# Top-32 attention and a gated feed-forward part on one core: weights used as they are split, half-batch groups, signs on ScalarE, sums divided out after the weighted values

## Chip, cores and metric

One core of a Trainium2 chip runs the whole kernel. The metric is device time in microseconds (us), lower is better, median of the runs. TensorE (PE in the profile) multiplies matrices, VectorE (DVE), ScalarE (ACT) and GpSimd (POOL) do the rest, and SyncE (SP) issues every DMA. PEld is TensorE's loading of weights, which overlaps its matmuls.

## What is computed

```python
scores = scale * np.matmul(q, k.transpose(0, 1, 3, 2))      # 8 batches, 8 heads, 576 x 576, depth 64
kth = np.partition(scores, -top_k, axis=-1)[..., -top_k:-top_k + 1]   # top_k = 32
scores = np.where(scores >= kth, scores, -1000000000.0)
attn = np.exp(scores - np.max(scores, axis=-1, keepdims=True))
attn = attn / (np.sum(attn, axis=-1, keepdims=True) + 1e-09)
x = (attn @ v) as 4608 rows x 512
gate = 1.0 / (1.0 + np.exp(-(x @ w_gate)))                  # w_gate, w_val 512 x 1536, in double precision
out = (gate * (x @ w_val) @ w_out).astype(np.float32)       # w_out 1536 x 512
```

## The kernel before, in words

The work is a list of 160 steps. A step is one tile of 128 query rows of a pair of heads (two head tiles, J = 2), or the last 64 rows of both heads in one tile (J = 1); there are 288 head tiles. Batches 0 and 1 go through in two halves (256 and 320 rows), batches 2 to 7 whole (576 rows): `groups`, line 55.

Per step, `scores` (L177) multiplies queries by keys, each as a leading part and a remainder, into PSUM, and ScalarE copies them out as `s` (L184). `select` finds each row's 32nd largest score on VectorE: the 8 largest of each of eight segments of 72 (L237), three rounds of 8 over those candidates (L241, L243), which give the 24th largest as a bound; a count of the scores that reach the bound (`over`, L248, which also writes 0 or 1 for each score); GpSimd takes `over` from `s` (L249), VectorE takes the 8 largest of what is left (L252) and picks the 32nd by the count (L253). ScalarE meanwhile takes the exponentials (L192). `normalise` masks and sums them on VectorE (L196), and ScalarE multiplies by one over the sum (L202). `turn` transposes the result on TensorE (L273, L278), ScalarE copies it to `et` (L274). For every two tiles `weigh` multiplies by the values: one 128-column matmul for the chunk that mixes both heads (L289), then pairs of 64-column matmuls, one for each head (L291, L292); ScalarE and GpSimd split the sum into two parts `xh`, `xl`.

The feed-forward part of a group (`ffn`) runs in units of at most 320 rows. A unit takes 432 matmuls: 12 times 24 with gate and value weights (`pz`, L331 to L333), each followed by tanh on ScalarE (L336), a multiply on VectorE (`gf`, L337) and a split into `gh`, `gl`; and 3 times 48 with the output weights (L351 to L353). Its weights come from DRAM through three buffers (L313), 18 loads of 1 MB for a group, shared by the two units of a 576-row group.

The weights arrive in double precision. `split_weights` (L98) turns all 18 tiles, as 36 halves, into two parts each and stores them to DRAM before any feed-forward work is written down; per half it takes three VectorE instructions (L126, L127, L130), ScalarE and GpSimd instructions, three matmuls (L134 to L136) and a store. Four halves can be in flight (`raws`, bufs=4), and the feed-forward pools take the memory of the split's pools afterwards.

What sets the order: the program writes the steps one after another, loads two to four steps ahead, and after each step as much of the feed-forward work as brings it to 640 rows behind the selection (`BEHIND`, `goal`). A scheduler then gives each engine a fixed sequence, in which feed-forward matmuls stand between those of the steps. Each engine runs its own sequence strictly in turn and waits on semaphores.

## Time and profile before

| what | value |
|---|---|
| median of 3 runs | 1690.8 us (1689.48 to 1691.35) |
| span of the profiled execution | 1685.6 us, 5.2 us under the median |
| PE busy, PEld busy | 1575.0 us (93%), 1398.7 us (83%) |
| DVE busy | 1521.8 us (90%) |
| ACT, POOL busy | 1166.2 us (69%), 1052.7 us (62%) |
| DMA | 297.37 MB, 176 GB/s over the span |

Only the profiled execution has rows, so terms are worked out against its 1685.6 us; the runs that were timed lie 5.2 us above it in the median. Busy time of PE is a model (matmuls overlap), so the distance from one matmul's start to the next says what a matmul costs, not its own duration.

### The profile page before, as it was taken

What the parts mean: (1) busy time and instruction counts of PE and PEld (TensorE: products, weight loads), DVE (VectorE), ACT (ScalarE), POOL (GpSimd) and SP (SyncE); (2) the same over time, 40 slices, a digit from 0 to 9 for tenths busy, and PEclk for the clock granted to TensorE, in tenths of its full rate; (3) what the DMA queues carried; (4) which work ended last, traced back from release to release, by engine and by line L of the source; (5) the groups of instructions that cost most, each with busy time, mean ns of one, the idle gap of its engine ahead of it and who ended that gap; (6) DMA issues with size and microseconds to landing.
All of it is one profiled execution on the core that took longest, in us unless ns stands there. A gap on an engine that the chain in (4) does not pass through costs nothing.

```text
span 1685.6 us, 36209 instructions
## 1 busy us (share of the span) xinstructions
PE 1575.0 (93%) x11506; PEld 1398.7 (83%) x11506; DVE 1521.8 (90%) x6802; ACT 1166.2 (69%) x2467; POOL 1052.7 (62%) x1187
## 2 busy tenths in 40 slices
PE   5665799999999989999999999999999999999998
PEld 2333598888989868998899999999999898999998
DVE  7999999999999999999999999999999999995000
ACT  7787777776777667776676767777776776765222
POOL 6766667767666766576764676576756675564233
PEclk8788899999999989999999999999999999999999
DMA  8777586756776543334433444434534353333543
GB/s 303 257 237 236 206 290 245 271 205 242 251 265 213 210 129 116 138 136 139 163 132 130 136 156 147 134 133 149 170 132 153 124 166 130 118 106 110 195 156 125
DMA packets 86026, 297.37 MB, mean 176 GB/s; under 512 B 9536, under 2 KB 38208, under 8 KB 62784
## 3 DMA queue, kind: packets, MB, share of 16 engines
q1 hardware_dynamic: 85824, 294.95, 51.1%
q8 instruction: 93, 1.52, 0.4%
q14 instruction: 109, 0.89, 0.2%
HBM read 266.60 MB, written 28.31 MB: 175 GB/s over the span
## 4 chain that ended last, share of the span: by engine, by line
PE 49%; DVE 35%; ACT 3%; issue 2%; POOL 1%; POOLq 0%; ACTq 0%; DVEq 0%
PE pz L332 8%; PE pz L331 8%; PE pz L333 8%; DVE e L196 7%; DVE cand L237 7%; DVE tops L252 5%; DVE over L248 5%; PE pss L177 5%; PE pt L273 4%; PE po L351 3%; PE po L353 3%; PE po L352 3%; DVE pick L253 3%; DVE tops L241 3%; PE po L292 3%; DVE cand L243 3%
## 5 line engine op out<-in xcount | busy, mean ns | idle before, releaser
L331 PE MATMUL pz<-xh,w 128*128 128x288 f32 (+2 forms) x1536 | 461.9, 301 | 3.1 <-DVE gf L337 1.5
L332 PE MATMUL pz<-xl,w 128*128 128x288 f32 (+2 forms) x1536 | 459.4, 299 | 0.1
L333 PE MATMUL pz<-xh,w 128*128 128x288 f32 (+2 forms) x1536 | 458.5, 299 | 0.0
L249 POOL TENSOR_TENSOR u<-s,over 128x1152 f32<-128x1152 f32 (+1 forms) x160 | 354.3, 2214 | 74.0 <-DVE over L248 70.2
L237 DVE MAX8 cand<-s 128x8 f32<-128x72 f32 x2304 | 355.3, 216 | 7.0 <-ACT s L184 6.7
L196 DVE SCALAR_TENSOR_TENSOR e<-s,st,e 128x576 f32<-128x576 f32 x288 | 300.8, 1065 | 0.1
L331 PEld LDWEIGHTS pz<-xh,w 128*128 128x128 f32 x1536 | 289.3, 188 | 9.0 <-issue 3.5
L332 PEld LDWEIGHTS pz<-xl,w 128*128 128x128 f32 x1536 | 289.2, 188 | 3.9 <-issue 3.5
L333 PEld LDWEIGHTS pz<-xh,w 128*128 128x128 f32 x1536 | 289.2, 188 | 2.7 <-issue 2.7
L202 ACT ACTIVATE e<-e,st 128x576 f32<-128x576 f32 x288 | 209.4, 771 | 83.1 <-DVE st L200 82.5
L339 POOL TENSOR_TENSOR gl<-gf,gh 128x288 fp32r<-128x288 f32 (+2 forms) x192 | 163.1, 850 | 153.7 <-ACT gh L338 145.8
L192 ACT ACTIVATE e<-s,st 128x576 f32<-128x576 f32 x288 | 210.2, 774 | 35.0 <-POOL st L190 34.1
L351 PE MATMUL po<-gh,w 128*128 128x288 f32 (+2 forms) x768 | 224.4, 302 | 6.3 <-DVE gf L337 3.9
L248 DVE TENSOR_SCALAR_CACHE_REDUCE over<-s,tops 128x576 bf16<-128x576 f32 x288 | 228.5, 798 | 1.1
L352 PE MATMUL po<-gl,w 128*128 128x288 f32 (+2 forms) x768 | 227.6, 299 | 0.6 <-POOL gl L339 0.5
L353 PE MATMUL po<-gh,w 128*128 128x288 f32 (+2 forms) x768 | 226.1, 297 | 0.0
L177 PE MATMUL pss<-k,qh 128*128 128x288 f32 (+2 forms) x672 | 199.7, 314 | 23.5 <-ACT s L184 16.4
L184 ACT ACTIVATE s<-pss 128x576 f32<-128x576 f32 x288 | 185.8, 645 | 47.2 <-PE pss L177 24.2
L252 DVE MAX8 tops<-u 128x8 f32<-128x576 f32 x288 | 204.3, 744 | 2.2 <-POOL u L249 1.4
L274 ACT ACTIVATE et<-pt 128x384 f32<-128x384 f32 x384 | 180.5, 491 | 35.5 <-PE pt L273 33.9
L273 PE MATMUL pt<-ident,e 128*128 128x128 f32 x1152 | 189.7, 281 | 7.7 <-ACT e L202 4.0
L177 PE MATMUL pss<-k,ql 128*128 128x288 f32 (+2 forms) x672 | 190.4, 302 | 0.4 <-POOL ql L159 0.4
(82 smaller groups left out, 3380.3 us busy)
## 6 DMA issues: line engine op xcount, KB each, us to landing
w<-ws SPq DMA_DIRECT2D x180, 1024.0 KB, 5.0
kraw<-in_k_dram SPq DMA_DIRECT2D x80, 288.0 KB, 3.2
qraw<-in_q_dram SPq DMA_DIRECT2D x160, 128.0 KB, 3.0
wraw<-in_w_dram SPq DMA_DIRECT2D x36, 512.0 KB, 5.0
ws<-wpair SPq DMA_DIRECT2D x36, 512.0 KB, 5.4
v<-in_v_dram SPq DMA_DIRECT2D x40, 352.0 KB, 3.8
out_dram<-acc SPq DMA_DIRECT2D x48, 144.0 KB, 2.3
out_dram<-acc SPq DMA_DIRECT2D x8, 160.0 KB, 4.1
```

The costliest lines, as they stand in the source:

```text
L177: nc.tensor.matmul(ps[:, half, o : o + n], x[:, h * P : (h + 1) * P], ks[h][:, k0 : k0 + n], start=t == 0, stop=t == len(todo) - 1,)
L196: nc.vector.scalar_tensor_tensor(e[:, j], s[:, j], kth[j], e[:, j], op0=ALU.is_ge, op1=ALU.mult, accum_out=st[:, 4 + j : 5 + j])
L237: nc.vector.max(cand[:, j, 8 * g : 8 * g + 8], s[:, j, g * SEG : (g + 1) * SEG])
L248: nc.vector.tensor_scalar(over[:, j], s[:, j], t, None, op0=ALU.is_ge, op1=ALU.add, accum_out=c)
L249: nc.gpsimd.tensor_tensor(u[:, :J], s[:, :J], over[:, :J], op=ALU.subtract)
L252: nc.vector.max(t, u[:, j])
L331: nc.tensor.matmul(ps, wt[:, u, 0, d], xh[:, cols], start=d == 0, stop=False)
L332: nc.tensor.matmul(ps, wt[:, u, 0, d], xl[:, cols], start=False, stop=False)
L333: nc.tensor.matmul(ps, wt[:, u, 1, d], xh[:, cols], start=False, stop=d == NP - 1)
L351: nc.tensor.matmul(ps, wt[:, e % 2, 0, f], gh, start=f == 0, stop=False)
L352: nc.tensor.matmul(ps, wt[:, e % 2, 0, f], gl, start=False, stop=False)
L353: nc.tensor.matmul(ps, wt[:, e % 2, 1, f], gh, start=False, stop=f == FG - 1)
```

## The change

- The two-part split is no longer a block of its own. `split_weight(idx, held)` splits one tile. Nine of the 18 are split during the eight steps of the first group: three of them straight into the feed-forward part's own weight buffers (`HELD`), six into DRAM (`LOADED`). The other nine are split when the first feed-forward unit asks for them, into its weight buffer, and also stored. Two halves can be in flight instead of four. The first scaling moves from ScalarE to VectorE, so VectorE has four instructions per half.
- All batches go in halves of 256 and 320 rows; a unit is a half, and each unit loads its own 18 weight tiles. Keys of a batch stay for its second half. `BEHIND` is 384 instead of 640, and the first unit may be written from 256 rows on.
- `over` on VectorE is replaced by a Sign on ScalarE that also sums the signs; the bound is read from a strip of saved bounds (`leads`) with its lower 16 bits left off. GpSimd multiplies instead of subtracting.
- ScalarE's multiply by one over the sum goes. GpSimd spreads that number over 128 columns (`inv`), TensorE transposes it (L329), ScalarE copies it out (`rs`), and VectorE multiplies it onto the weighted values (L335, L339).
- In `weigh` the pairs come first, from the last chunk down, and the mixed matmul last.

```diff
-    groups = [(b, *half) for b in range(2) for half in ((0, 2), (2, NT + 1))]
-    groups += [(b, 0, NT + 1) for b in range(2, B)]
+    groups = [(b, *half) for b in range(B) for half in ((0, 2), (2, NT + 1))]
-    BEHIND = 640
+    BEHIND = 384
+    HELD, LOADED = 3, 6
...
-    bk = ctx.enter_context(tc.tile_pool(name="bk", bufs=4))
+    bk = ctx.enter_context(tc.tile_pool(name="bk", bufs=2 * NP))
...
+    pre_pools = {n: pre.enter_context(tc.tile_pool(name=n, bufs=bufs)) for n, bufs in (("signs", 1), ("raw", 2), ("parts", 2))}
...
+    def split_weight(idx, held):
+        if held:
+            wt = pools["w"].tile([P, 2, 2, NP, P], F32R, tag="w", name=f"wsplit_{idx}")
+            ready[idx] = wt
...
-                    nc.scalar.activation(lead, top.bitcast(F32), AF.Copy, scale=2.0**-112)
+            nc.vector.tensor_scalar(lead, top.bitcast(F32), 2.0**-112, None, op0=ALU.mult)
...
-        for j in range(J):
-            nc.scalar.activation(e[:, j], e[:, j], AF.Copy, scale=st[:, 6 + j : 7 + j])
+        inv = bi.tile([P, P], F32, tag="inv", name=f"inv_{nm}")
+        nc.gpsimd.tensor_copy(
+            inv.rearrange("p (j d) -> p j d", j=J), st[:, 6 : 6 + J].unsqueeze(2).to_broadcast([P, J, P // J])
+        )
...
-            nc.vector.tensor_scalar(over[:, j], s[:, j], t, None, op0=ALU.is_ge, op1=ALU.add, accum_out=c)
-        nc.gpsimd.tensor_tensor(u[:, :J], s[:, :J], over[:, :J], op=ALU.subtract)
+            nc.scalar.activation(
+                under[:, j], s[:, j], AF.Sign, bias=bound, scale=-CUT, accum_out=sums[:, j : j + 1]
+            )
+        nc.gpsimd.tensor_tensor(u[:, :J], s[:, :J], under[:, :J], op=ALU.mult)
...
-            nc.tensor.matmul(po, mixed, et[:, 4, :n], start=True, stop=False)
-            for c in range(4):
-                nc.tensor.matmul(po[:D], vt[:, c], et[:, c, :n], start=False, stop=c == 3)
-                nc.tensor.matmul(po[D:], vt[:, 6 + c], et[:, 5 + c, :n], start=False, stop=c == 3)
+            for c in reversed(range(4)):
+                nc.tensor.matmul(po[D:], vt[:, 6 + c], et[:, 5 + c, :n], start=c == 3, stop=False)
+                nc.tensor.matmul(po[:D], vt[:, c], et[:, c, :n], start=c == 3, stop=False)
+            nc.tensor.matmul(po, mixed, et[:, 4, :n], start=False, stop=True)
...
+        for t, inv in enumerate(invs):
+            nc.tensor.transpose(rb[:, t * P : (t + 1) * P], inv, ident)
+        nc.scalar.activation(rs[:, :m], rb[:, :m], AF.Copy)
...
-        nc.scalar.activation(xf, po, AF.Copy)
+            nc.vector.tensor_tensor(xf, po, rs[:, :n], op=ALU.mult)
...
+            if not (general or idx in stored):
+                split_weight(idx, True)
...
+            goal = max(at - BEHIND, min(at - 2 * P, 2 * P))
```

TensorE's sequence before, in the middle of batch 3: a `weigh` (po) with its mixed matmul first.

```order
L289 MATMUL po_3_1_3_11270<-et_3_0_3_11104,v_5_3_10761 128x256
L291 MATMUL po_3_1_3_11270<-et_3_0_3_11104,v_5_3_10761 64x256
L292 MATMUL po_3_1_3_11270<-et_3_0_3_11104,v_5_3_10761 64x256
L291 MATMUL po_3_1_3_11270<-et_3_0_3_11104,v_5_3_10761 64x256
L332 MATMUL pz_4_2_3_0_0_11650<-xl_4_1_6591,w_4_11_11646 128x288
L177 MATMUL pss_4_0_0_1_11529<-k_6_0_1_11511,qh_4_0_0_11189 128x288
L177 MATMUL pss_4_0_0_1_11529<-k_6_0_1_11511,ql_4_0_0_11190 128x288
L177 MATMUL pss_4_0_0_1_11529<-k_6_0_1_11511,qh_4_0_0_11189 128x288
L177 MATMUL pss_4_0_0_1_11529<-k_6_0_1_11511,ql_4_0_0_11190 128x288
L333 MATMUL pz_4_2_3_0_0_11650<-xh_4_1_6590,w_4_11_11646 128x288
L292 MATMUL po_3_1_3_11270<-et_3_0_3_11104,v_5_3_10761 64x256
```

Other matmuls stand between the first and the second head's half of one chunk: the pair is broken. The end of a `weigh` at the same stage of the changed kernel (inv is the spread-out number, pt are the next transposes):

```order
L318 MATMUL po_3_3_2_11993<-et_3_2_2_11838,v_7_2_11458 64x256
L319 MATMUL po_3_3_2_11993<-et_3_2_2_11838,v_7_2_11458 64x256
L320 MATMUL po_3_3_2_11993<-et_3_2_2_11838,v_7_2_11458 128x256
L329 MATMUL po_3_3_2_11993<-ident_102,inv_3_2_2_11834 128x128
L329 MATMUL po_3_3_2_11993<-ident_102,inv_3_3_2_11976 128x128
L304 MATMUL pt_3_4_2_0_12146<-ident_102,e_3_4_2_12118 128x128 x3
L307 MATMUL pt_3_4_2_1_12152<-ident_102,e_3_4_2_12118 64x128
L377 MATMUL pz_6_1_1_0_0_12178<-xh_6_0_9627,w_6_5_12174 128x256
```

Four whole pairs, the mixed matmul and two transposes now stand together (in 62 of 64 `weigh`s; before, 59 of 64 had the pair broken).

TensorE's sequence before, where the first feed-forward unit (po2_0) ends and the second (pz_1) begins:

```order
L351 MATMUL po2_0_2_3_0_4346<-gh_0_2_3_0_4149,w_0_17_4327 128x256
L352 MATMUL po2_0_2_3_0_4346<-gl_0_2_3_0_4150,w_0_17_4327 128x256
L353 MATMUL po2_0_2_3_0_4346<-gh_0_2_3_0_4149,w_0_17_4327 128x256
L331 MATMUL pz_1_0_0_0_0_4441<-xh_1_0_1756,w_1_0_4437 128x320
L332 MATMUL pz_1_0_0_0_0_4441<-xl_1_0_1757,w_1_0_4437 128x320
```

The same place in the changed kernel:

```order
L396 MATMUL po2_0_2_3_0_3156<-gl_0_2_0_0_2525,wsplit_17_3104 128x256
L147 MATMUL wrest_17_1_3125<-wt_frac_17_1_3126,plus_159 128x512
L299 MATMUL pt_1_1_2_0_4140<-ident_102,e_1_1_2_4095 128x128 x3
L299 MATMUL pt_1_1_2_1_4145<-ident_102,e_1_1_2_4095 128x128 x3
L375 MATMUL pz_1_0_0_0_0_3682<-xh_1_0_1418,w_1_0_3678 128x320
L376 MATMUL pz_1_0_0_0_0_3682<-xl_1_0_1419,w_1_0_3678 128x320
```

The split of the last weight tile (wrest_17) now stands right ahead of the second unit; before, all 36 halves stood ahead of the first.

VectorE's sequence before, in the selection of batch 4 (`over` of one tile between rounds of others):

```order
L241 MAX tops_4_4_2_13958<-cand_4_4_2_13957 128x8
L248 TENSOR_SCALAR over_4_4_2_13963,counts_115<-s_4_4_2_13617,tops_4_4_2_13958 128x576
L237 MAX cand_4_0_3_14065<-s_4_0_3_13781 128x8 x2
L252 MAX tops_4_3_2_13795<-u_4_3_2_13799 128x8 x2
L237 MAX cand_4_0_3_14065<-s_4_0_3_13781 128x8 x6
```

And in the changed kernel, in batch 6:

```order
L266 MAX leads_119<-cand_6_0_2_19732 128x8
L279 MAX below_6_1_1_19549<-u_6_1_1_19554 128x8 x2
L219 RECIPROCAL st_6_0_1_19392<-st_6_0_1_19392 128x2
L381 SCALAR_TENSOR_TENSOR gf_11_0_0_0_19488<-gf_11_0_0_0_19488,pz_11_0_0_0_1_19475 128x320
L280 SCALAR_TENSOR_TENSOR pick_6_1_1_19552,kths_118<-wanted_107,sums_6_1_1_19551,below_6_1_1_19549 128x8
L335 TENSOR_TENSOR xf_6_1_0_19282<-po_6_1_0_19268,rs_6_1_0_19280 128x256
```

The pass over 576 scores is gone from VectorE, and the multiply onto the weighted values (xf) is there instead, once for two tiles.

## Rows read from the trace of the kernel before

**Rows 1.** The page's part 1: busy us (share of the span), instructions.

```profile
PE 1575.0 (93%) x11506; PEld 1398.7 (83%) x11506; DVE 1521.8 (90%) x6802; ACT 1166.2 (69%) x2467; POOL 1052.7 (62%) x1187
```

**Rows 2.** Windows of 50 us: length, each engine's busy us (instructions), PE clock, DMA share, GB/s.

```profile
150.00:200.00 50.00, 30.47 (x121) 18.63 (x121) 50.00 (x179) 37.62 (x71) 30.24 (x29) 0.86 0.59 202
...
550.00:600.00 50.00, 48.49 (x349) 44.30 (x349) 50.00 (x230) 34.82 (x73) 33.68 (x38) 1.00 0.60 212
600.00:650.00 50.00, 39.67 (x261) 30.72 (x260) 49.97 (x233) 33.31 (x70) 32.97 (x36) 0.86 0.36 113
650.00:700.00 50.00, 50.00 (x389) 46.28 (x388) 49.94 (x246) 40.03 (x86) 30.19 (x36) 1.00 0.41 138
...
1550.00:1600.00 50.00, 50.00 (x387) 47.80 (x386) 3.78 (x9) 13.79 (x35) 13.12 (x18) 1.00 0.49 172
```

**Rows 3.** TensorE in order of time: start us, duration us, instruction, count.

```profile
294.49 0.28 PE L353 MATMUL po<-gh,w 128*128 128x256 f32 x1
294.61 0.31 PE L331 MATMUL pz<-xh,w 128*128 128x320 f32 x1
...
295.35 0.31 PE L333 MATMUL pz<-xh,w 128*128 128x320 f32 x1
...
997.06 0.49 PE L273 MATMUL pt<-ident,e 128*128 128x128 f32 x3
997.38 0.60 PE L289 MATMUL po<-et,v 128*128 128x256 f32 x2
...
998.92 0.66 PE L278 MATMUL pt<-ident,e 128*128 128x128 f32 x4
...
1000.96 0.43 PE L292 MATMUL po<-et,v 128*64 128x256 f32 x1
...
1002.40 0.30 PE L281 MATMUL pt<-ident,e 128*64 128x128 f32 x1
...
1009.93 0.30 PE L351 MATMUL po<-gh,w 128*128 128x288 f32 x1
...
1010.72 0.29 PE L351 MATMUL po<-gh,w 128*128 128x288 f32 x1
...
1086.48 0.59 PE L289 MATMUL po<-et,v 128*128 128x256 f32 x2
...
1088.88 0.55 PE L278 MATMUL pt<-ident,e 128*128 128x128 f32 x3
```

**Rows 4.** VectorE in order of time: start us, duration us, instruction, count.

```profile
301.65 0.47 DVE L337 SCALAR_TENSOR_TENSOR gf<-gf,pz 128x320 f32<-128x320 f32 x1
...
1000.01 0.81 DVE L248 TENSOR_SCALAR_CACHE_REDUCE over<-s,tops 128x576 bf16<-128x576 f32 x1
...
1000.75 1.26 DVE L196 SCALAR_TENSOR_TENSOR e<-s,st,e 128x576 f32<-128x576 f32 x1
```

**Rows 5.** Groups by line: count | busy us, mean ns of one | idle before.

```profile
L248 DVE TENSOR_SCALAR_CACHE_REDUCE over<-s,tops 128x576 bf16<-128x576 f32 x288 | 228.5, 798 | 1.1
...
L337 DVE SCALAR_TENSOR_TENSOR gf<-gf,pz 128x288 f32<-128x288 f32 (+2 forms) x192 | 84.5, 440 | 117.4 <-PE pz L333 114.9 <-ACT qh L158 2.3
...
L132 POOL TENSOR_TENSOR wt_frac<-wt_frac,wt_lead 128x512 fp32r<-128x512 f32 x36 | 50.6, 1410 | 33.5 <-DVE wt_lead L130 26.4 <-DVE cand L237 2.9 <-PE wrest L134 1.9
...
L127 DVE SCALAR_TENSOR_TENSOR wt_bits<-wraw,wt_lead 128x512 uint32<-128x512 uint32 x36 | 39.3, 1091 | 0.0
...
L126 DVE TENSOR_SCALAR wt_lead<-wt_lead 128x512 uint32<-128x512 uint32 x36 | 27.9, 776 | 10.4 <-ACT wt_lead L125 10.4
...
L130 DVE TENSOR_SCALAR wt_lead<-wt_bits 128x512 uint32<-128x512 uint32 x36 | 18.0, 507 | 0.0
```

**Rows 6.** Waits of TensorE from 200 us on: waiter, line, releaser: us in total, times, longest.

```profile
PE po L351 <- DVE gf L337: 3.9, 4, 1.1
```

**Rows 7.** Waits of SyncE's DMA queue: us in total, times, longest.

```profile
SPq L116 <- DVE wt_bits L127: 51.6, 20, 5.4
```

**Rows 8.** The page's part 6: DMA issues, KB each, median us to landing.

```profile
w<-ws SPq DMA_DIRECT2D x180, 1024.0 KB, 5.0
```

More of the change, by code (lines that the diff above doesn't have):

```diff
@@ L23 @@
 LOWEST = -3.0e38
+CUT = 1.0 + 2.0**-23
 @with_exitstack
@@ new lines, in tile_topk_attention_then_gated_ffn @@
+    for name, bufs in (("w", 3), ("f2", 3), ("f4", NE + 1), ("fg", FG + 2)):
+        pools[name] = ctx.enter_context(tc.tile_pool(name=name, bufs=bufs))
+    order = []
+    for g in range(NG):
+        order += [g * FG + f for f in range(FG)] + [NF + g * (NE // 2) + e for e in range(NE // 2)]
+    ready, stored = {}, set()
+    pre = ExitStack()
+    pre_pools = {n: pre.enter_context(tc.tile_pool(name=n, bufs=bufs)) for n, bufs in (("signs", 1), ("raw", 2), ("parts", 2))}
+    plus, minus = [pre_pools["signs"].tile([P, P], F32R, tag=t, name=t) for t in ("plus", "minus")]
@@ L233, in select @@
         u = b2.tile([P, 2, S], F32, tag="u", name=f"u_{nm}")
-        over = b3.tile([P, 2, S], BF16, tag="over", name=f"over_{nm}")
+        under = b2.tile([P, 2, S], BF16, tag="under", name=f"under_{nm}")
         for j in range(J):
@@ L371, in fetch @@
                 g, p, _ = steps[m]
-                keys[g, p] = load_keys(groups[g][0], p, f"{mark}{g}_{p}")
+                b, first, _ = groups[g]
+                if first == 0:
+                    keys[b, p] = load_keys(b, p, f"{mark}{g}_{p}")
+                values[g, p] = load_values(b, p, f"{mark}{g}_{p}")
         def begin(m):
@@ L396, in run @@
             b, first, end = groups[g]
+            if not general and g == 0:
+                n = m * (HELD + LOADED) // (2 * NP)
+                for t in range(n, (m + 1) * (HELD + LOADED) // (2 * NP)):
+                    split_weight(order[t], t < HELD)
+                    stored.add(order[t])
             fetch(m + FETCH)
```

168 lines of the change are left out of this document (89 added, 79 removed).

## The prediction

> **What bounds the kernel now.** I read the page's busy shares first, then the windows by stage, then TensorE's starts. The shares name no single bound: PE is busy 93% of the span, DVE 90%, ScalarE and GpSimd under 70% [rows 1]. The windows separate three stages [rows 2]. From 150 to 200 us VectorE is busy 50.00 of 50 us and PE only 30.47, at a clock of 0.86: selection and the splitting of the weights hold VectorE, and the feed-forward part has not begun. In the middle both are full (PE 48.49, DVE 50.00 from 550 to 600). From 1550 us VectorE has 3.78 us of work per window and PE 50.00: the last feed-forward rows run alone. One hole stands in the middle: from 600 to 650 us PE is busy 39.67 us and issues 261 matmuls where the windows beside it have 349 and 389; the half batches' feed-forward work is used up and the first 576-row group is not ready.
>
> Is PE really full in the middle, or only labelled so? The distance from start to start tells: 288 columns take (1010.72 - 1009.93) / 6 = 0.132 us each in the middle [rows 3], 320 columns (295.35 - 294.61) / 5 = 0.148 us, 256 columns 0.12 us (294.49 to 294.61). These are the columns at full clock with little between, and PE's waits for `gf`, the result that VectorE returns to it, sum to 3.9 us after 200 us [rows 6]. So from about 200 us on, **PE is the bound and VectorE is within a few per cent of it**. It follows that VectorE's relief alone is worth little. The end is: the time T1 at which PE begins the second feed-forward unit, plus the PE work left from there. Before, T1 = 294.61 [rows 3] and 1685.6 - 294.6 = 1391.0 us are left.
>
> The Trainium skill, "Perfetto Trace Analysis", section "Identifying the Most-Contended Engine", says that a matmul row's busy share doesn't measure PE's headroom and LDWEIGHTS busy does. Here that is 83%, which would leave VectorE at 90% as the engine to relieve; the spacing above disagrees, and the rival "VectorE was the bound" below is what that reading would give.
>
> **T1, term by term.** Until T1 VectorE is full, so VectorE's queue sets it. It returns the first `gf` of the second unit at 301.65 [rows 4]. In the changed sequence the last split instruction stands right before the second unit, so I count what VectorE does up to it.
> - Out: 44 `over` instructions stood ahead of that `gf`. One takes 1000.75 - 1000.01 = 0.74 us [rows 4]: -32.6.
> - In, selection that the new order puts earlier: the counts by line are 416 segment maxima against 376 and 46 maskings against 41, so 5 head tiles more. A head tile costs (1521.8 - 85.2 for the splits (39.3 + 27.9 + 18.0) - 84.5 for `gf`) / 288 = 4.69, less 0.74 without `over`: 3.95 us [rows 1, 5]; +19.8.
> - In, the scaling moved from ScalarE: 36 instructions over 512 numbers, which read every second word. The trace has none on VectorE. The nearest are L130 (507 ns), L126 (776) and L127, which reads the same words and a second tensor (1091) [rows 5]. I take L126's, a one-input instruction under the same disturbance: +27.9, between 18.3 and 39.3. L140 now also reads every second word; if it goes from 507 to 776 ns, +9.7, which I leave for the range.
> - In, the multiply onto the weighted values: 10 of 256 columns and 8 small ones. `gf` is the nearest, one operand in PSUM, 440 ns [rows 5]: at most 7.9; I take +5.
>
> The sum is +20.1: VectorE is through with the splits at 321.8. Then come GpSimd's 1.41 us [rows 5], a matmul and a ScalarE copy, some 3 us together: **T1 = 325**. The first unit itself starts earlier, since only half of the splits stand ahead of it, but it ends later: its last weight tile is split within it. ScalarE's lost `lead` step is no gain here, as ScalarE has slack.
>
> **PE's work from T1 on**, against 1391.0 us.
> - Already done by T1, as the new order has PE 4 steps further: 32 score matmuls at 0.132, 39 transposes at (997.38 - 997.06) / 3 = 0.107, 2 `weigh`s at 2.4 [rows 3]: -13.2.
> - Whole pairs in `weigh`: a broken one takes (998.92 - 997.38) + (1002.40 - 1000.96) = 2.98 us, one of the few unbroken ones 1088.88 - 1086.48 = 2.40 [rows 3]. 54 are left: 54 x 0.58 = -31. The mixed matmul's new place at the end may cost or save 0.1 each.
> - Transposes of `inv`: 136 left x 0.107 = +14.6. If they don't pipeline, up to 0.16 each (a lone group of three lasts 0.49 us [rows 3]): +22.
> - Units of 256 and 320 columns in place of two of 288, in six batches: 0.120 + 0.148 - 0.264 = 0.004 us for each of 2592 pairs: +10.4.
> - The hole at 600 us goes, since groups are halves throughout: 369 - 261 = 108 matmuls x 0.132 = -14.
> - PE's waits for `gf`: at most -3.9, with VectorE at (1521.8 - 213 + 35 + 28) / 1678 = 82% of its time (the terms of the third rival). I count -4.
>
> Left: 1353. ScalarE gains a Sign per head tile and loses the multiply by one over the sum, as many passes over 576 numbers; GpSimd gains 160 short copies and loses the subtractions for keys that were loaded twice. Both stay near their 69% and 62% [rows 1] and hide behind PE. 276 weight loads in place of 180, 1 MB each, land in about 5.0 us [rows 8], three at a time, beside at least 432 x 0.12 = 52 us of PE for 18 of them; the half batches before ran so already, at a DMA share of 0.60 [rows 2]. Where that cover failed, PE would wait per tile.
>
> **Forecast:** 325 + 1353 = 1678 in the profiled execution, against 1685.6; with the 5.2 us by which the median lies above it, **1683 us**, 0.5% under 1690.8. Its own range: T1 from 315 (18.3 for the scaling) to 335, `inv` up to +7, hence 1673 to 1697; the likeliest part of it is below 1690.8. A measurement of this kernel tells about 0.2%, 3.4 us, from no change.
>
> **Rivals.**
> - *T1 comes later, and the kernel is slower.* Everything after T1 is PE's, so each microsecond of T1 is one at the end. VectorE reaches T1 in 325 only if it never waits. Two raw buffers instead of four stand in a queue where SyncE already waits 51.6 us for them with four [rows 7]; half of that on VectorE is 25 us, and L140's 9.7 may join. Against it: VectorE was full throughout with four, and half of the splits are now spread over the first unit. It decides from T1 = 336 on. At T1 = 350: 1708, range 1694 to 1728.
> - *Interleaving wins.* The first unit starts earlier by what half of the splits take on VectorE (18 x 2.37 = 43 us), and if the splits that it still needs stand in gaps of VectorE's queue, T1 stays near 295 and PE's early idle time shrinks: 295 + 1353 + 5 = 1653, range 1640 to 1670. For it: 19.5 of the 50 us before 200 are idle on PE [rows 2]. Against it: VectorE has no gaps there (50.00 of 50). The skill's same page, "Optimization Strategy", advises to interleave stages with different bounds; by it this case would hold, and the 50.00 speaks against it.
> - *VectorE was the bound.* It is through before 1550 [rows 2]. Less 288 x 0.74 = 213, plus some 35 for the new multiplies (64 large at 0.44, 64 small) and 28 for the scaling: 1400; then the 545 matmuls that stand behind the last transposes at 0.148 = 81: 1481, so 1486. PE's own work from T1 forbids it, unless the spacings are themselves waits.
> - *It does not do what it says.* A bound without its lower bits could put a row's count outside 24 to 31, and all is computed again in the general way: over 3000. With the reference's draw the counts stay between 24 and 30.
> - *Weight loads bind.* With 96 MB more, PE waits for tiles: at 0.1 us for each of 276, 28 us more: 1711, range to 1740.
>
> **How the numbers follow.** Forecast 0.42 (of it 0.28 faster by over 0.2%, 0.12 within, 0.02 slower); later T1 0.31; interleaving 0.19; VectorE the bound 0.03; computed again 0.02; loads 0.03. Faster: 0.28 + 0.19 + 0.03 = 0.50. Within 0.2%: 0.12. Slower: 0.02 + 0.31 + 0.02 + 0.03 = 0.38. The range 1648 to 1718 leaves out about a fifth of that: the two small extremes, half of the loads, and the ends of the two rivals beside the forecast.
>
> **What would show it.** T1 is the start of the first 320-column `pz` in the new trace: 325 here, under 305 for interleaving, over 336 for slower. Before it VectorE should be full in each window; idle time there on DMA of raw weights is the slower rival. From T1 to the end 1353 us should pass, with starts 0.12 and 0.148 apart, a `weigh` of 2.4 us, no hole near 600 us, and a tail without VectorE of about 80 us. New waits of PE for `et`, `rs` or weight tiles of more than 25 us in all would break the second half of the sum.

## The result, and the profile after

The changed kernel takes **1700.6 us** (median of 4 runs, 1699.4 to 1702.6), the kernel before in the same comparison 1690.1 (1688.4 to 1691.4): a ratio of 1.0063, with a 95% interval of 1.0049 to 1.0077. It is slower by 0.6%. I had forecast 1683, faster by 0.5%, and a slower kernel at 0.38. The profiled execution spans 1698.7 us against 1685.6.

Part 1 of the page, to be read beside [rows 1] (busy us, share of the span, instructions):

```profile
PE 1575.7 (93%) x11666; PEld 1424.5 (84%) x11666; DVE 1397.1 (82%) x6389; ACT 1167.7 (69%) x2703; POOL 1085.5 (64%) x1331
```

VectorE lost 125 us of work, ScalarE stayed, GpSimd got 33; TensorE is as busy as before, in a longer span. Windows of the new trace, as in [rows 2], one added from 350 us:

```profile
150.00:200.00 50.00, 46.96 (x348) 42.71 (x347) 43.33 (x185) 33.94 (x79) 30.61 (x37) 0.90 0.56 196
...
350.00:400.00 50.00, 48.55 (x336) 46.10 (x336) 24.93 (x94) 25.73 (x60) 26.16 (x32) 1.00 0.69 258
...
600.00:650.00 50.00, 48.85 (x418) 46.43 (x419) 42.08 (x220) 38.46 (x95) 36.46 (x47) 1.00 0.88 295
...
1550.00:1600.00 50.00, 50.00 (x437) 47.36 (x436) 44.73 (x224) 35.91 (x86) 29.36 (x42) 1.00 0.68 242
```

TensorE is now well filled from 150 to 200 us and the hole at 600 us is closed. But VectorE is not full ahead of T1 (43.33 of 50), idles half of the window from 350 us, and its selection still runs at 1550 us, where it was over before.

The start of the second feed-forward unit, in TensorE's rows in order of time (start us, duration, line, instruction, idle before):

```profile
329.97 0.28 PE L396 MATMUL po<-gl,wsplit 128*128 128x256 f32 x1
330.38 0.50 PE L147 MATMUL wrest<-wt_frac,plus 128*128 128x512 f32 x1
331.75 1.18 PE L299 MATMUL pt<-ident,e 128*128 128x128 f32 x6 [0.86 <-DVE e L215]
332.69 0.39 PE L375 MATMUL pz<-xh,w 128*128 128x320 f32 x1
```

T1 is **332.7**, after 294.6 [rows 3] and a forecast of 325. The two stages by windows, first of the kernel before and then of the changed one (columns as in [rows 2]):

```profile
0.00:294.61 294.61, 214.81 (x1188) 154.23 (x1189) 283.90 (x1097) 226.07 (x449) 196.22 (x201) 0.89 0.74 254
294.61:1685.60 1390.99, 1360.16 (x10320) 1244.46 (x10318) 1237.87 (x5706) 940.10 (x2020) 856.44 (x987) 0.99 0.47 160
```

```profile
0.00:332.69 332.69, 245.44 (x1310) 176.57 (x1310) 310.25 (x1215) 233.27 (x498) 208.81 (x234) 0.85 0.54 183
332.69:1698.70 1366.01, 1330.22 (x10359) 1247.95 (x10358) 1086.86 (x5176) 934.39 (x2206) 876.67 (x1098) 1.00 0.70 250
```

T1 came 38.1 us later, and 1366.0 us were left instead of 1391.0: 25.0 less. The difference is the 13.1 us of the spans. Seen from the end: the last mask of the selection starts at 1602.4 (the row below) instead of 1541.7, 60.6 us later, and what follows it takes 96.4 us instead of 143.9. The forecast had a tail of about 80. In the kernels below that have the new groups it is 92 to 97 us, in the others 134 to 144.

```profile
1602.36 0.82 DVE L215 SCALAR_TENSOR_TENSOR e<-s,kths,e 128x576 f32<-128x576 f32 x1
```

**How I count pauses.** Busy rows of a pipelined TensorE can hide short waits, so I went through the starts of its matmuls: each distance from one start to the next of over 0.33 us counts as a pause, by what it exceeds 0.15. 0.15 is about one product and 0.33 about two; both limits are choices of mine. The span less all pauses is called *products* below. All kernels of this study, by their profiled executions, in us:

| kernel | median | span | T1 | pauses to T1 | pauses behind | products |
|---|---|---|---|---|---|---|
| before | 1690.1 | 1685.6 | 294.6 | 133.3 | 33.8 | 1518.5 |
| changed | 1700.6 | 1698.7 | 332.7 | 150.2 | 36.5 | 1512.0 |
| b_weigh_order | 1678.8 | 1679.1 | 290.4 | 134.0 | 60.9 | 1484.2 |
| a_old_weigh | 1719.5 | 1717.6 | 324.5 | 139.0 | 28.8 | 1549.8 |
| a_scale_act | 1689.0 | 1689.3 | 321.2 | 140.9 | 33.4 | 1515.0 |
| a_raw3 | 1682.5 | 1681.9 | 297.6 | 127.7 | 41.9 | 1512.3 |
| a_bits | 1686.2 | 1685.4 | 304.1 | 131.7 | 42.1 | 1511.6 |
| a_raw3_scale | 1677.0 | 1676.3 | 304.5 | 125.2 | 36.5 | 1514.6 |
| a_split_first | 1731.2 | 1729.8 | 383.7 | 180.0 | 34.6 | 1515.2 |
| b_raw2 | 1687.7 | 1684.8 | 342.8 | 153.4 | 12.6 | 1518.8 |
| b_sign | 1731.9 | 1731.3 | 299.6 | 130.9 | 68.7 | 1531.7 |
| b_sign_weigh | 1719.7 | 1717.0 | 290.4 | 129.8 | 87.1 | 1500.1 |
| a_normalise | 1711.3 | 1710.0 | 334.2 | 155.4 | 52.5 | 1502.1 |
| b_inv | 1706.7 | 1704.9 | 280.7 | 119.5 | 45.6 | 1539.8 |
| a_split_before | 1670.1 | 1671.1 | 275.0 | 125.7 | 35.8 | 1509.6 |
| a_sb_raw2 | 1687.3 | 1683.4 | 322.2 | 142.3 | 31.4 | 1509.7 |

Names with b_ are the kernel before with an edit, names with a_ the changed one. The medians are of the timed runs and the spans of one profiled execution each, so differences of the two can disagree by some us. The change took 6.5 us off TensorE's products and added 19.6 us of pauses, 16.9 of them ahead of T1.

### The profile page after: what moved, and what is told of

It reads as the page before. It is cut to its first block, busy times and chain, and to the rows that moved or that the text cites. A ratio compares the mean times of both kernels' runs of the same rounds, so it can differ in the third digit from the quotient of the medians.

```text
span 1698.7 us, 36838 instructions
## 1 busy us (share of the span) xinstructions
PE 1575.7 (93%) x11666; PEld 1424.5 (84%) x11666; DVE 1397.1 (82%) x6389; ACT 1167.7 (69%) x2703; POOL 1085.5 (64%) x1331
## 5 line engine op out<-in xcount | busy, mean ns | idle before, releaser
L375 PE MATMUL pz<-xh,w 128*128 128x320 f32 (+1 forms) x1472 | 445.0, 302 | 2.6 <-DMA w<-ws 0.7
L376 PE MATMUL pz<-xl,w 128*128 128x320 f32 (+1 forms) x1472 | 441.9, 300 | 0.0
L377 PE MATMUL pz<-xh,w 128*128 128x320 f32 (+1 forms) x1472 | 440.1, 299 | 0.0
L277 POOL TENSOR_TENSOR u<-s,under 128x1152 f32<-128x1152 f32 (+1 forms) x160 | 353.2, 2209 | 75.8 <-ACT under L274 73.5
L215 DVE SCALAR_TENSOR_TENSOR e<-s,kths,e 128x576 f32<-128x576 f32 x288 | 283.2, 1001 | 3.1 <-ACT e L210 3.0
L274 ACT ACTIVATE under<-s,leads 128x576 bf16<-128x576 f32 x288 | 223.1, 775 | 70.7 <-DVE leads L266 57.7
L279 DVE MAX8 below<-u 128x8 f32<-128x576 f32 x288 | 205.0, 747 | 61.5 <-POOL u L277 60.2
L383 POOL TENSOR_TENSOR gl<-gf,gh 128x256 fp32r<-128x256 f32 (+1 forms) x192 | 165.4, 862 | 133.4 <-ACT gh L382 127.0
L395 PE MATMUL po<-gh,w 128*128 128x320 f32 (+1 forms) x736 | 216.6, 308 | 6.0 <-DVE gf L381 3.9
L396 PE MATMUL po<-gl,w 128*128 128x320 f32 (+1 forms) x736 | 218.8, 302 | 2.9 <-POOL gl L383 2.9
L397 PE MATMUL po<-gh,w 128*128 128x320 f32 (+1 forms) x736 | 216.4, 299 | 0.0
L202 ACT ACTIVATE s<-pss 128x576 f32<-128x576 f32 x288 | 185.7, 645 | 30.4 <-PE pss L195 21.8
L299 PEld LDWEIGHTS pt<-ident,e 128*128 128x128 f32 x1152 | 141.7, 143 | 50.8 <-DVE e L215 33.2
```

The source lines that it names most:

```text
L215: nc.vector.scalar_tensor_tensor(e[:, j], s[:, j], kth[j], e[:, j], op0=ALU.is_ge, op1=ALU.mult, accum_out=st[:, 4 + j : 5 + j])
L277: nc.gpsimd.tensor_tensor(u[:, :J], s[:, :J], under[:, :J], op=ALU.mult)
L279: nc.vector.max(below[:, j], u[:, j])
L299: nc.tensor.transpose(pt[:, c], ef[:, k0 : k0 + P], ident)
L375: nc.tensor.matmul(ps, wt[:, u, 0, d], xh[:, cols], start=d == 0, stop=False)
L376: nc.tensor.matmul(ps, wt[:, u, 0, d], xl[:, cols], start=False, stop=False)
```

## Experiments

Ratios are to the kernel before, with 95% intervals.

### The order in weigh, alone and undone

b_weigh_order puts only this into the kernel before; a_old_weigh takes it out of the changed one.

```diff
-            nc.tensor.matmul(po, mixed, et[:, 4, :n], start=True, stop=False)
-            for c in range(4):
-                nc.tensor.matmul(po[:D], vt[:, c], et[:, c, :n], start=False, stop=c == 3)
-                nc.tensor.matmul(po[D:], vt[:, 6 + c], et[:, 5 + c, :n], start=False, stop=c == 3)
+            for c in reversed(range(4)):
+                nc.tensor.matmul(po[D:], vt[:, 6 + c], et[:, 5 + c, :n], start=c == 3, stop=False)
+                nc.tensor.matmul(po[:D], vt[:, c], et[:, c, :n], start=c == 3, stop=False)
+            nc.tensor.matmul(po, mixed, et[:, 4, :n], start=False, stop=True)
```

> The kernel before, with one thing of the change: in weigh the eight half-width products run first, in pairs and downwards, and the mixed one last. Theory P (TensorE is the bound before, so the end is T1, the start of the second feed-forward unit, plus TensorE's work): in the profile of the changed kernel a weigh took 9 x 0.1351 = 1.22 us against 9 x 0.1654 = 1.49 before, after T1; 112 of them x 0.27 = 30 us come off the end: 1660, ratio 0.982. Rival V (VectorE, busy 50 of 50 us in nearly every window before, paces the middle and TensorE's products only fill it): the last mask still comes near 1541, the feed-forward rest behind it is as long, and the time stays at 1690 within 4.

(That text takes nine rows of the trace for a weigh; a weigh has 18, and 56 of them lie behind T1. The product is the same.)

Measured: 0.9934 (0.9918 to 0.9951), 10.6 us faster (6.5 by the two profiled spans): outside V's 4 us, but nearer to V than to P. The products fell by 34 us in the table, and the pauses rose by 28. The windows split at its T1 show the same: 1360.16 us busy became 1335.62, in a stage only 2 us shorter.

```profile
290.40:1679.10 1388.70, 1335.62 (x10325) 1246.04 (x10324) 1241.70 (x5716) 937.14 (x2027) 861.87 (x986) 0.99 0.46 160
```

VectorE did as much as before in that stage (1241.70 and 1237.87), and its last mask came at 1537.4 instead of 1541.7. About half of the new pauses wait for `gf`, the result that VectorE returns (waiter, releaser: us in total, times, longest; behind T1, first in this run and then in the kernel before):

```profile
PE pz L331 <- DVE gf L337: 15.1, 14, 1.8
```

```profile
PE pz L331 <- DVE gf L337: 1.5, 2, 1.0
```

**TensorE's spacing at full clock in [rows 3] was right, and still TensorE was not what paced the kernel before:** it had matmuls enough to fill its time, and with less to do it mostly waited more.

> The changed kernel with weigh in the old order: the mixed product first, then the halves. Put into the kernel before, the new order took 29 us of products off TensorE and gave 27 us of them back as new pauses. Theory V (before, VectorE paced the middle; in the changed kernel it is busy 80% there and TensorE is the bound): here the 29 us come back in full, 1725 to 1732. Rival (the pauses take up whatever TensorE's products gain or lose, in both kernels): at most 10 us more, under 1711.

Measured: 1.0186 (1.0169 to 1.0203), 19 us slower than the changed kernel: between the two, nearer to V. Products +38, pauses -19. With VectorE relieved, the order in weigh is worth about half of its products; before, a third.

### Where T1 comes from

The first scaling back on ScalarE (a_scale_act):

```diff
-            nc.vector.tensor_scalar(lead, top.bitcast(F32), 2.0**-112, None, op0=ALU.mult)
+            nc.scalar.activation(lead, top.bitcast(F32), AF.Copy, scale=2.0**-112)
```

> The changed kernel, with the 36 multiplies of the leading words by a power of two on ScalarE again, as in the kernel before. Theory T (the loss is T1, and T1 is VectorE's queue): the 36 multiplies took 30.5 us on VectorE ahead of T1 = 332.7; without them T1 is about 303 to 306 and the kernel 27 to 30 us shorter: 1672, ratio to the kernel before 0.989. Rival W (T1 is held by the chain raw load, VectorE, ScalarE, GpSimd, TensorE of the splits, two at a time): ScalarE in the chain costs what VectorE saves, T1 stays above 325 and the time above 1693.

Measured: 0.9994 (0.9984 to 1.0003), T1 321.2. 30 us off VectorE's queue moved T1 by 11.5 and the time by 11.6: neither theory. VectorE's busy time ahead of T1 fell by 26.4 us, and its idle time there rose from 22.4 to 37.4, as it now waits for ScalarE's scaling and for scores (`cand <- ACT s` 12.2 us, 1.6 before the edit). VectorE's sum alone does not set T1.

```profile
0.00:321.24 321.24, 233.21 (x1292) 170.78 (x1292) 283.86 (x1159) 245.85 (x521) 206.88 (x230) 0.87 0.55 189
```

Three raw buffers instead of two (a_raw3; a line not shown leaves one buffer instead of two for the finished pairs, which pays for the memory):

```diff
-    pre_pools = {n: pre.enter_context(tc.tile_pool(name=n, bufs=bufs)) for n, bufs in (("signs", 1), ("raw", 2), ("parts", 2))}
+    pre_pools = {n: pre.enter_context(tc.tile_pool(name=n, bufs=bufs)) for n, bufs in (("signs", 1), ("raw", 3), ("parts", 2), ("pairs", 1))}
```

> The changed kernel with three raw buffers for the weights in place of two (one buffer less for the finished pair pays for it). Theory T (VectorE's queue alone): VectorE idled 22 us before T1, 13 of them on raw loads of which 9 are the start; at most 10 us can come back: T1 322 to 330, time 1690 to 1699. Rival W (the two buffers also set the order: VectorE selects ahead while it waits for a split's chain): with three the split instructions come earlier in VectorE's queue, 42 maskings instead of 50 stand ahead of the second unit's first gf, T1 falls by about 28 to 305, and the time to 1672 to 1680, since about 7 us of what VectorE put ahead has its TensorE work still to come.

Measured: 0.9960 (0.9946 to 0.9974), 18.1 us under the changed kernel, T1 297.6: W, 2 us over its range in time. Its first stage in windows:

```profile
0.00:297.60 297.60, 224.97 (x1202) 165.59 (x1203) 281.98 (x1081) 211.78 (x450) 201.48 (x218) 0.85 0.58 201
```

Against the changed kernel's 310.25 us ahead of T1, VectorE does 28.3 us less work there, and idles 15.6 us instead of 22.4. **The two buffers cost little as idle time; they cost as other work put ahead.** The order of VectorE's queue is fixed beforehand, and where the split can't have a buffer, selection stands in its place: 48 maskings ahead of T1 with two buffers, 40 with three, 40 in the kernel before. That is why the waits for raw weights looked harmless. VectorE's own waits ahead of T1 in the changed kernel (waiter, releaser: us in total, times, longest):

```profile
DVE wt_lead L137 <- DMA wraw<-in_w_dram: 14.7, 6, 9.3
DVE gf L381 <- PE pz L377: 2.8, 2, 1.5
```

9.3 of the 14.7 are the first load. All splits first, none in the unit (a_split_first):

```diff
-    HELD, LOADED = 3, 6
+    HELD, LOADED = 3, 15
```

> The changed kernel with all 18 weights split in the first group of rows, none within the first feed-forward unit (15 and not 6 loaded back). Theory T: splitting within the unit is no loss; with all splits first, 59 maskings stand ahead of the second unit's first gf instead of 50, T1 moves from 333 to about 360 and the time to 1715 to 1725. Rival I (splitting within the unit is what lost the time, because the first unit then waits for each split): T1 falls to about 320 or under and the time to 1685 to 1690.

Measured: 1.0247 (1.0230 to 1.0264), T1 383.7, against I. The size is beyond T's. With two raw buffers, splitting half of the weights within the unit is better than all of them ahead of it.

Two buffers, but the shifted word in a tile of its own, as before (a_bits; here too the finished pairs keep one buffer, and some lines are left out):

```diff
...
+            word = pre_pools["parts"].tile([P, NP * P], F32, tag="word", name=f"wt_word_{idx}_{i}")
-            nc.vector.scalar_tensor_tensor(top, top, 0x80000000, lead_u, op0=ALU.bitwise_and, op1=ALU.bitwise_or)
+            nc.vector.scalar_tensor_tensor(word_u, top, 0x80000000, lead_u, op0=ALU.bitwise_and, op1=ALU.bitwise_or)
...
-            bits = top.bitcast(F32)
+            bits = word
```

> The changed kernel, two raw buffers as in it, but the shifted word goes into a tile of its own instead of back into the raw buffer (one finished-pair buffer less pays for it, the same memory as the run with three raw buffers). Theory H (what cost T1 was that a raw buffer stays held until ScalarE and TensorE have read the word in it): the buffer comes free after VectorE's third instruction, 43 maskings instead of 50 stand ahead of the second unit's first gf, T1 is 298 to 310 and the time 1682 to 1690. Rival N (only the number of buffers for loads matters): T1 stays over 325 and the time over 1696.

Measured: 0.9981 (0.9972 to 0.9991), T1 304.1: H. In the changed kernel the word goes back into the raw buffer, which then stays taken until ScalarE and TensorE have read it. A third buffer or an early release do nearly the same. Three buffers and the scaling on ScalarE together (a_raw3_scale):

> The changed kernel with three raw buffers and the scaling of the leading words on ScalarE. In the order 48 to 50 maskings stand ahead of the second unit's first gf where three buffers alone have 42, and VectorE's work ahead of it is about 286 us against 290. Theory T: T1 stays within 5 us of 297, but 8 head tiles more are done by then, 1.5 us of TensorE's work each: 1667 to 1674. Rival (work that is done ahead of T1 pays nothing, only T1 does): 1680 to 1684.

Measured: 0.9924 (0.9907 to 0.9941), T1 304.5: between the two. T1 is later than with three buffers alone, and the kernel 5.5 us faster, so work done ahead of T1 pays in part.

### The same shortage in the kernel before

b_raw2 gives the kernel before two raw buffers.

```diff
-                for n, bufs in (("signs", 1), ("raw", 4), ("parts", 4))
+                for n, bufs in (("signs", 1), ("raw", 2), ("parts", 4))
```

> The kernel before with two raw buffers for the weights in place of four, nothing else. Theory W (two buffers make the splits come late in VectorE's queue): 54 maskings stand ahead of the second unit's first gf instead of 41, VectorE's work ahead of it is 341 us instead of 286, T1 moves from 295 to about 340 to 350, and with 13 head tiles of 1.5 us of TensorE's work done ahead the time is 1705 to 1725. Rival (loads land in 4 us, two buffers are enough where the word leaves them early): 1688 to 1695.

Measured: 0.9992 (0.9982 to 1.0001). **T1 moved by 48 us, as W said, and the time not at all**, where W had 15 to 35 us more. TensorE's rows give T1, VectorE's the last mask, first here and then in the kernel before:

```profile
342.78 0.31 PE L331 MATMUL pz<-xh,w 128*128 128x320 f32 x1
```

```profile
1541.82 0.82 DVE L196 SCALAR_TENSOR_TENSOR e<-s,st,e 128x576 f32<-128x576 f32 x1
```

```profile
1541.73 0.82 DVE L196 SCALAR_TENSOR_TENSOR e<-s,st,e 128x576 f32<-128x576 f32 x1
```

The pauses moved from behind T1 (33.8 to 12.6) to ahead of it (133.3 to 153.4), with nearly the same sum (167.1 and 166.0). VectorE is nearly full to the end of the selection in both (1217.9 us before and 1205.5 here of the 1240 from 300 to 1540); 51 maskings instead of 40 were done by T1, and these it had not to do later. My "each microsecond of T1 is one at the end" was false for the very kernel that I took it from.

### What the relief of VectorE is worth

b_sign puts only the Sign into the kernel before, with what belongs to it (the strip of bounds, GpSimd's multiply, and two buffers for the signs where `over` had three); b_sign_weigh adds the order in weigh. Lines left out are marked.

```diff
-            nc.vector.tensor_scalar(over[:, j], s[:, j], t, None, op0=ALU.is_ge, op1=ALU.add, accum_out=c)
-        nc.gpsimd.tensor_tensor(u[:, :J], s[:, :J], over[:, :J], op=ALU.subtract)
...
+            nc.scalar.activation(under[:, j], s[:, j], AF.Sign, bias=bound, scale=-CUT, accum_out=sums[:, j : j + 1])
+        nc.gpsimd.tensor_tensor(u[:, :J], s[:, :J], under[:, :J], op=ALU.mult)
```

> The kernel before with the comparison with the lead moved from VectorE to ScalarE as a Sign (the product with it on GpSimd, the 32nd largest from the count of signs), and nothing else: the weights are split up front, the scaling by one over the sum stays on ScalarE. Theory V: VectorE loses 288 x 0.74 = 213 us; T1, its queue's, falls by about 44 x 0.74 = 32 us to 263; of the 34 us of pauses behind T1 ten or so go: 1645 to 1655, ratio 0.976. Rival S (ScalarE, 1166 us busy before, gets 223 us more and is 82% busy in a long chain): what VectorE gives, TensorE waits for the scaled weights instead: 1680 or more.

Measured: 1.0252 (1.0235 to 1.0269), 43 us slower: S's side, far over its 1680. T1 is 299.6, not V's 263. Part 1 of its page, then waits of TensorE and of VectorE, and VectorE's last mask:

```profile
PE 1595.7 (92%) x11506; PEld 1407.2 (81%) x11506; DVE 1376.4 (80%) x6225; ACT 1361.1 (79%) x3043; POOL 1062.9 (61%) x1187
```

```profile
PE pss L179 <- ACT s L186: 25.1, 23, 2.5
...
PE pt L281 <- ACT et L282: 14.1, 16, 5.2
...
PE pt L281 <- ACT e L204: 7.8, 8, 1.9
```

```profile
DVE cand L243 <- ACT s L186: 94.7, 69, 4.3
DVE below L260 <- POOL u L258: 67.5, 54, 4.1
```

```profile
1597.14 0.82 DVE L198 SCALAR_TENSOR_TENSOR e<-s,kths,e 128x576 f32<-128x576 f32 x1
```

No engine is over 80% besides TensorE, and the kernel is slower than with VectorE at 90%. ScalarE now stands in the chain of a head tile five times (scores, exponentials, Sign, scaling, copies of the transposes), each pass 0.5 to 0.8 us in one queue, and both neighbours wait for it: TensorE's waits for copied scores went from 16.4 to 25.1 us, for `et` from 3.5 to 14.1, VectorE's for scores from 6.7 to 94.7. For the scaled weights, which S named, they are 7.8 us after 4.0. The last mask comes 55 us later than in the kernel before, although VectorE has 145 us less to do. TensorE's pauses rose by 32.5 us, its products by 13. That the longer chain is the cause is read from these waits; the one buffer less for the signs was not tried apart.

> The same as the run with the Sign alone, and the new order in weigh too. Theory V (VectorE and TensorE were both within a few per cent of the bound, so each relief pays only with the other): the products' 29 us are added to what the Sign alone brings, where the new order alone brought 11: 1616 to 1626, under both kernels by over 60 us. Rival S (ScalarE's longer chain takes VectorE's place): the two together bring no more than the Sign alone and 10 us.

Measured: 1.0187 (1.0170 to 1.0204), 12 us under b_sign: S, 2 us over its range.

a_normalise takes the spread sums out of the changed kernel (its edit is shown, without the part in `weigh`), and b_inv puts only them into the kernel before:

```diff
-        nc.gpsimd.tensor_copy(
-            inv.rearrange("p (j d) -> p j d", j=J), st[:, 6 : 6 + J].unsqueeze(2).to_broadcast([P, J, P // J])
-        )
+        for j in range(J):
+            nc.scalar.activation(e[:, j], e[:, j], AF.Copy, scale=st[:, 6 + j : 7 + j])
...
```

> The changed kernel with the scaling by one over the sum on ScalarE again, over all keys, ahead of the transposes, and no spread sums. TensorE loses 144 transposes (14 us), VectorE 64 large and 64 small multiplies (35 us), ScalarE gets 288 passes of 0.77 us (222 us). Theory S (the Sign pays only because the scaling left ScalarE; with both on it, as in the run of before with the Sign, the pauses of TensorE grow from 37 to about 70 us): 1715 to 1735. Rival P (TensorE's products decide): 1686 to 1692.

Measured: 1.0129 (1.0112 to 1.0145), 10.7 us slower than the changed kernel: S's direction, 4 us short of its range. Products -10.0, pauses +21.3.

> The kernel before with the sums spread and applied late, and nothing else: ScalarE loses 222 us, VectorE, which is full until 1540, gets 35 us, TensorE 144 transposes (14 us). Theory V (before, VectorE paces the selection): the last mask moves by 30 to 40 us and the time to 1710 to 1730. Rival S (the chain through ScalarE paced it as much): the last mask comes no later and the time is 1680 to 1700.

Measured: 1.0100 (1.0083 to 1.0117); the last mask came 19 us later. V's direction, below its sizes. Windows up to the last mask, first of the kernel before and then of b_inv:

```profile
0.00:1542.60 1542.60, 1438.19 (x10465) 1264.34 (x10466) 1509.66 (x6774) 1126.65 (x2373) 1010.49 (x1133) 0.97 0.52 178
```

```profile
0.00:1561.40 1561.40, 1459.45 (x10622) 1287.34 (x10623) 1532.06 (x6899) 957.67 (x2087) 1082.54 (x1292) 0.97 0.51 176
```

VectorE got 22.4 us more to do, ScalarE 169 us less, and the stretch grew by 18.8. That follows VectorE's work, but TensorE's products rose by as much (21.2), so this run does not tell the two apart. The Sign alone costs 43 us, the spread sums alone 17, while taking the spread sums out of the changed kernel, which has the Sign, costs 10.7: the two work as a pair that takes from ScalarE what it gives to it.

### The split as before, the rest as changed

a_split_before takes the whole first part of the change back (18 tiles split ahead of the loop by the block of before, all units load their weights) and keeps the rest; a_sb_raw2 is that with two raw buffers. The block itself is left out below.

```diff
...
+        if not general:
+            split_weights()
+            ffn_pools()
+            bxs.append(ctx.enter_context(tc.tile_pool(name="bx1", bufs=NP)))
         todo, work, at, col = [], 0, 0, 0
...
-            if not (general or idx in stored):
-                split_weight(idx, True)
```

> The changed kernel with the whole first part of the change undone: all weights are split ahead of the selection's loop with the block of before (four raw buffers, words in their own tile, scaling on ScalarE), and loaded back by every unit; Sign, spread sums, kept keys, halves and the order in weigh stay. Theory G (what the kernel lost is the place and the buffers of the split; behind T1 VectorE has room now, so an earlier T1 counts): 38 maskings stand ahead of the second unit's first gf instead of 50 and VectorE's work there is 242 us instead of 318; T1 falls to 255 to 270, ten head tiles of 1.5 us of TensorE's work fall behind it: 1640 to 1660. Rival S (with the Sign, ScalarE is in the way while it splits, as in the run of before with the Sign alone, where T1 did not fall at all): T1 295 or more, 1675 to 1695.

Measured: **1670.1 us, 0.9879 (0.9862 to 0.9895)**, the fastest kernel here, 1.2% under the one before. T1 is 275.0, 5 over G's range, and the time 10 over it; S is refuted by T1 and by the time. Its first stage:

```profile
0.00:275.00 275.00, 193.95 (x1105) 143.19 (x1106) 243.56 (x876) 208.59 (x438) 179.32 (x197) 0.86 0.73 258
```

Between it and the changed kernel lie 30.5 us, and by spans 27.6: 2.4 of products and 25.2 of pauses. **The first part of the change costs about 30 us, and the rest gains 20.** The first part is more than the place of the split: it also has two raw buffers instead of four, the word kept in the raw buffer, and the scaling on VectorE. In the rest, the half-batch groups and kept keys were not tried by themselves.

> The same with two raw buffers in place of four, nothing else. In the kernel before this edit moved T1 from 295 to 343 and the time not at all. Theory G (before, VectorE is busy without a break to the end of the selection, so what it does ahead of T1 it has not to do later; here it has room behind T1, and a later T1 is lost time): 48 maskings instead of 38 ahead, T1 about 35 to 45 us later, the time 15 to 30 us longer than with four. Rival (T1 never counts, only TensorE's pauses in all): within 5 us of the run with four.

Measured: 0.9989 (0.9979 to 0.9998), 17.3 us slower than with four; T1 322.2, +47. G, with T1 2 us over its range. The edit that cost nothing in the kernel before costs 17 us here, more than half of the 30. The windows behind T1, first with four buffers and then with two:

```profile
275.00:1671.10 1396.10, 1361.98 (x10564) 1274.57 (x10562) 1127.47 (x5478) 980.36 (x2302) 912.87 (x1135) 0.99 0.69 246
```

```profile
322.20:1683.40 1361.20, 1331.17 (x10365) 1250.45 (x10363) 1086.20 (x5197) 935.33 (x2209) 879.36 (x1096) 0.99 0.70 251
```

Of the 47 us of T1, 35 come back behind it, since more products stand ahead. What does not come back are pauses: here +16.6 us ahead of T1 and only -4.4 behind it, in the kernel before +20.1 and -21.2. The reading that fits, though no run isolates it, is VectorE's room: in the kernel before it has 1237.87 us of work behind T1 in the 1247 us to its last mask, so that maskings done early shorten that stretch; here it has 1086.20 in 1268 us, up to a last mask at 1590, and they don't.

**What the place of the split costs by itself is much less than 30 us.** With two raw buffers and a tile for the word, the interleaved split (a_bits, scaling on VectorE) takes 1686.2 us and the block ahead (a_sb_raw2, scaling on ScalarE) 1687.3. With more buffers and the scaling on ScalarE in both, the interleaved one (a_raw3_scale, three buffers) takes 1677.0 and the block (a_split_before, four and a tile for the word) 1670.1. A pair that differs in the place alone was not run.

## Why the prediction was wrong, point by point

**What bounds.** "PE is the bound and VectorE is within a few per cent of it" was the step that failed first. Full spacing showed that TensorE had work, not that it set the pace: 34 us off its products brought 10.6 (b_weigh_order), and 48 us of T1 brought none (b_raw2). What these two runs point to is VectorE, busy 50 of 50 us, which the prediction had set aside; no run took work off VectorE without giving it to another engine, and the one that gave it to ScalarE was slower (b_sign). In the changed kernel it is neither alone: 38 us of products cost 19 (a_old_weigh).

**T1.** Forecast 325, measured 332.7. VectorE was through with the last split instruction at 328.9, forecast 321.8. Counted from start to start, as the forecast counted `over`, VectorE's work up to there was 15.6 us more than up to the `gf` of before, where the sum had +20.1:
- `over` -31.9 (forecast -32.6); selection +17.4 (+19.8), with 416 maxima and 46 maskings, as counted.
- The 36 multiplies 27.7 (27.9), the multiplies onto the weighted values 4.9 (5), the other split instructions -2.7 (not in the sum). L140 took 0.9 more than L130 had, so of the 9.7 left to the range almost nothing came.
- VectorE idle: 22.4 us (332.69 - 310.25) against 10.7 (294.61 - 283.90), all of it ahead of the last split instruction. The sum had no such term, by "VectorE was full throughout with four"; that is the term missed, +11.7. That T1 was off by only 8 us is in part luck: the work was put 4.5 us too high. The 46 maskings were taken from the changed order, so what the two buffers put ahead was in the sum, but not known for a cost of the two buffers.

The two lines of the new trace (count | busy us, mean ns | idle before; the busy time counts each instruction whole, also where the next one had begun):

```profile
L137 DVE TENSOR_SCALAR wt_lead<-wraw 128x512 f32<-128x512 f32 x36 | 30.4, 846 | 14.7 <-DMA wraw<-in_w_dram 14.7
...
L140 DVE TENSOR_SCALAR wt_lead<-wraw 128x512 uint32<-128x512 uint32 x36 | 19.2, 534 | 0.0
```

**Work left from T1.** Forecast 1353, measured 1366.0. Times between starts behind T1, without pauses, before and after:
- Already done by T1: -13.2 forecast; 32 scores, 39 transposes and 2 weighs, -13.8.
- Whole pairs: -31 forecast; 1008 rows at 0.162 became 972 at 0.135, -26. The pairs start together, mostly 0.21 us apart, and a weigh lasts 1006.27 - 1003.86 = 2.41, as forecast:

```profile
1003.86 0.43 PE L318 MATMUL po<-et,v 128*64 128x256 f32 x1 [0.47 <-ACT et L300]
1003.86 0.43 PE L319 MATMUL po<-et,v 128*64 128x256 f32 x1
1004.12 0.38 PE L318 MATMUL po<-et,v 128*64 128x256 f32 x1
1004.13 0.38 PE L319 MATMUL po<-et,v 128*64 128x256 f32 x1
1004.34 0.38 PE L318 MATMUL po<-et,v 128*64 128x256 f32 x1
1004.34 0.38 PE L319 MATMUL po<-et,v 128*64 128x256 f32 x1
1004.55 0.38 PE L318 MATMUL po<-et,v 128*64 128x256 f32 x1
...
1005.73 0.70 PE L320 MATMUL po<-et,v 128*128 128x256 f32 x2
1006.27 0.38 PE L329 MATMUL po<-ident,inv 128*128 128x128 f32 x2
```

- Transposes of `inv`: +14.6 forecast, 136 at 0.094: +12.7. The dearer +22 did not come.
- Units of 256 and 320 columns: +10.4 forecast, about +5.
- The hole and the waits for `gf`: **-18 forecast, +2.7 measured.** This is the mis-sized term. The pauses from 600 to 800 us did fall, from 16.6 to 9.1, but from 800 to 1400 they rose from 7.4 to 18.3. They are short and spread; about 15 of the 36.5 us stand ahead of transposes, and half of that is waiting for masks (`pt <- DVE e`, 7.6 us). A hole that closes in one place is not time gained when the waits come up again elsewhere.
- What I had not counted: transposes came 0.005 us closer together, -6.

Without the pauses the second half of the sum would have been better than forecast by 8 us; with them it was 13 worse. The forecast's own range also has a slip in its sum: 1683 with 10 for T1 and 7 for `inv` is 1700, not 1697.

**The rivals.** The one that came true is "T1 comes later"; that the two raw buffers hold T1 back is shown by a_raw3, a_bits and a_sb_raw2. Its point of decision, T1 = 336, was taken from the 1353 us and lay too high: 332.7 was enough. Its evidence was the wrong quantity: it looked for idle time of VectorE on loads, and most of the cost stood in the order as selection put ahead. "Interleaving wins" is refuted for the kernel as it stands (T1 332.7, not under 305); with three buffers T1 is 297.6 and the time 1682.5, still over its 1670, and in neither of the two pairs above did the interleaved split win clearly. The Trainium skill, "Perfetto Trace Analysis", section "Optimization Strategy", advises to interleave stages with different limits; here both the split and the selection are VectorE's, and the nearest pair of runs, a_bits and a_sb_raw2, comes out alike. The same section says that repeated gaps on an engine can mean too few buffers; the runs agree on the buffers (18 us for a third), though the gap in the trace was only some 12 us more than before. "VectorE was the bound" fits the kernel before better than the forecast did, and its 1486 still did not come: in the changed kernel VectorE idles 215 us up to its last mask, and TensorE's products alone stand at 1512. "Weight loads bind" is refuted: TensorE's waits for `w` behind T1 are 1.4 us in all, and a load lands in 5.2 us, after 5.0 in [rows 8]. The general computation was not run.

**What stays open.** How much of a microsecond of T1 counts in the changed kernel: 35 us brought 18 (a_raw3), 47 cost 17 (a_sb_raw2), 11.5 brought 11.6 (a_scale_act). The head tiles done ahead explain part; I have no rule for it. Nor was it tried what holds the pauses behind T1 at 29 to 42 us in the kernels that have the changed selection on both engines.

## What to carry to other kernels

A saturated matmul stream shows that TensorE has work, not that it paces: before pricing a saving there, take a few per cent off it alone and see whether the end moves. Where a program's order is fixed beforehand, too few buffers show less as waits than as other work ahead of the delayed step, so compare what stands ahead of it in the queue, not the idle time. And price two edits that trade work between the same engines as a pair: here the one alone cost 43 us and the other 17. A change that bundles several edits is taken apart before one of them is blamed: the new split cost 30 us, and the number of buffers alone 17 (a_sb_raw2).

## What the runs showed of the hardware that I had not expected

Transposes of the spread sums come 94 ns apart behind the full-width product and 115 ns (15.6 us for 136) where the half-width products stand right ahead of them, in a_old_weigh. The multiply that reads every second word (L137) took 0.40 to 0.54 us in 24 of its 36 times and 0.90 to 2.58 in the other 12, so the stride alone does not make it dear. In each of those 12 GpSimd was in an instruction with two inputs (`u`, `ql` or `wt_frac`) when the multiply began, and the multiply ended 0.28 us after GpSimd's instruction did, so it stood waiting for it. The 12 took 20.2 of the 30.4 us. Two of VectorE's rows, without and with the wait, and GpSimd's row beside the second (38.62 + 2.37 = 40.99, and 38.97 + 2.30 = 41.27):

```profile
9.30 0.43 DVE L137 TENSOR_SCALAR wt_lead<-wraw 128x512 f32<-128x512 f32 x1 [9.30 <-DMA wraw<-in_w_dram]
...
38.97 2.30 DVE L137 TENSOR_SCALAR wt_lead<-wraw 128x512 f32<-128x512 f32 x1 [2.04 <-DMA wraw<-in_w_dram]
```

```profile
38.62 2.37 POOL L277 TENSOR_TENSOR u<-s,under 128x1152 f32<-128x1152 f32 x1
```

In b_sign ScalarE was busy only 79% of the span, and the kernel was 43 us slower; a share of that size on an engine that stands several times in one head tile's chain was no sign of room.
